# Two weight quarters for the first batch before the second batch, first weights at the head of the queue, blocks of 512 and 384

## The chip, the cores and the metric

The kernel runs on one core of one Trainium2 chip. The metric is the device time of one execution in microseconds.

## What is computed

An attention over 32 memory slots per head, whose output passes through two feed-forward layers of width 2048. There are 8 batches of 576 tokens (4608 tokens in all), 8 heads of 64.

```python
def _attn_ref(q, k, v, phi):
    a = softmax over the sequence of phi          # 8 x 8 x 576 x 32
    k_m = einsum('bhsm,bhsd->bhmd', a, k);  v_m = einsum('bhsm,bhsd->bhmd', a, v)
    attn = softmax(q @ k_m.T / 8)                 # over the 32 slots
    return attn @ v_m

x = attn_out as 4608 x 512
h = x @ w1_in;  g = where(h > 0, h, exp(min(h, 0)) - 1);  x = g @ w1_out
h = x @ w2_in;  g = h * clip(h + 3, 0, 6) / 6;            return g @ w2_out
```

All four weights arrive as 64-bit floats, 512 x 2048 or 2048 x 512 each.

## The kernel before

**Units of the first layer.** Each batch is cut into two halves of 288 tokens; a half is a unit `u`, there are 16. The width 2048 is cut into 16 slices of 128, in four quarters of four slices. An item is one slice of one unit: `first(n)` makes six TensorE products into `ph` (L662 to L664), `middle(n)` applies the activation on ScalarE (L671, L673, L680), VectorE (L675) and GpSimd (L682), and `second(n)` makes twelve products into the four banks `acc` (L706). Each product with full precision is three products of high and low parts.

**What an item waits for.** `first` needs the unit's attention weights `a` (high part L592, low part on GpSimd L595) and the folded weights `w` of its batch and quarter: `fold` multiplies the summary of the batch by the quarter of `w1i` (L616), and takes high and low parts (L622, L624). `second` needs the same quarter of `w1o`.

**The weights.** A quarter is four tiles of 1 MB: two of `w1i`, two of `w1o`. `fetch` loads one (L240), `convert` turns 64-bit floats into 32-bit ones: absolute value on ScalarE (L284), scaled low word on ScalarE (L287), four steps on VectorE (L289, L291, L294, L297), a product on GpSimd (L310), and a last addition on VectorE (L312). For `w1o` a high part on ScalarE (L317) and a low part on GpSimd (L321) follow. The very first two tiles are converted in single slices of 512 elements, the others in pairs of 1024.

**The attention of a batch.** `front_first` (batch 0) or `front` makes the exponentials of `phi`; `summary` makes `pkv` (L515), `kvn` (L527), a transposition, and the copies `vt` (VectorE, L537) and `kt` (ScalarE, L539); `scores` (L552) and `softmax` (L568 to L599) give `a`, per half.

**Order of the items.** For the first two batches (units 0 to 3) `items` runs through the quarters, and in each through all four units, so that a new quarter of weights is wanted every 16 items; the sums over quarters are kept in SBUF (L736 to L755). From the third batch on, all 16 slices of a unit follow one another. While layer one runs, the second layer's weights are converted and written back to DRAM (`seven`).

**The second layer** works on blocks of token pairs: `BLOCKS = [464] * 4 + [448]`, each `t` meaning 2t tokens. Seven products per weight tile replace eight; a block makes 14 x 8 groups of six products of `t` columns (`product1`, L858 to L860; `product2`, L885 to L887) and streams its weights anew.

**The order of every engine's instructions** comes from a planner that runs while the program is built. Each task yields pieces with an engine, an estimated cost and the keys and buffer slots they need; every lane has a due time, counted in items; the planner gives an engine the piece with the smallest due time, and fills gaps with others (`Schedule.pick`). The due times come from `first_use` and `AHEAD`. A key `("step", n)` holds a piece back until item `n` has made its first products; the key `("e", 0, 0)` holds it back until the first half of batch 0's exponentials is there. On the chip the order of each engine is fixed; only waits on semaphores remain. All loads are issued by SyncE, in one queue, in the order of the lists `loads` and `fetches`.

Of the kernel before, what the change touches and what calls it, by code (L numbers as in the profile page):

```python
# [36 lines left out]

BLOCKS = [464] * 4 + [448]
NU = len(BLOCKS)
# [9 lines left out]

ORDER = (1, 6, 2, 7, 5, 4, 3)  # L50

READ = 12
# [128 lines left out]
def mixer(ctx, tc, phi_t, phi_n, kv, q_t, w1i, w1o, w2i, w2o, out):  # L181
# [83 lines left out]
    def convert(n, c, name, i, f, how, *keys):  # L265
# [42 lines left out]
        for x in range(m):  # L308
            yield Piece("pool", 1.2)
            pool.tensor_tensor(out=rest[:, x], in0=rest[:, x], in1=highf[:, x], op=ALU.mult)  # L310
        yield Piece("dve", two)
        dve.tensor_tensor(out=top, in0=top, in1=rest, op=ALU.add)  # L312
        drop(n, c)
# [148 lines left out]
    def front_first(b):  # L462
# [8 lines left out]
        for g in range(NG):  # L471
            yield Piece("dve", 0.7, ("pt", b, g))
            pt.append(kept.pop((b, "pt", g)))
            dve.tensor_reduce(out=nmax[:, g:g + 1], in_=pt[g], op=ALU.max, axis=AX.X, negate=True)
            yield Piece("act", 0.76)
            act.activation(out=pt[g], in_=pt[g], func=ACTF.Exp, bias=nmax[:, g:g + 1],
                           accum_out=sums[:, g:g + 1])
            yield Piece("pe", 1.0, slots=("h", "bank"))
            many, few = new("h", [P, SC - 1, P], "pt4"), new("bank", [P, P], "pt1")
            for c in range(SC):  # L480
                n = P if c < SC - 1 else last
                to = many[:, c] if c < SC - 1 else few[:n]
                pe.transpose(to, pt[g][:, c * P:c * P + n], ident)
            give("x")
            give("t")
            to = pn[:, :, g * P:(g + 1) * P]
            yield Piece("dve", 0.65, early=READ)
            dve.tensor_copy(to[:, :SC - 1], many)
            give("h")
            yield Piece("dve", 0.25, early=READ)  # L490
            dve.tensor_copy(to[:last, SC - 1], few[:last])
            give("bank")
            mark("e", b, g)
# [7 lines left out]
    def summary(b, g, whole):  # L501
# [33 lines left out]
        kr, vr = slice(64 * g, 64 * g + 64), slice(64 - 64 * g, 128 - 64 * g)  # L535
        yield Piece("dve", 0.25, early=READ)
        dve.tensor_copy(vt[b % 2][vr], v4[vr])  # L537
        yield Piece("act", 0.25, early=READ)
# [95 lines left out]

    UB = 2 * HV
    items = [(u, f, q) for q in range(NQ) for u in range(UB) for f in range(q * FQ, q * FQ + FQ)]
    items += [(u, f, None) for u in range(UB, NB) for f in range(FC)]
# [203 lines left out]
    def product1(u, j, i):  # L841
# [6 lines left out]
        if after:  # L848
            keys.append((after, u, j))
        yield Piece("pe", 1.375 * t / 512, *keys, slots=(kind,) if begin else ())  # L850
        if begin:
# [17 lines left out]
    def product2(u, i, j):  # L869
# [6 lines left out]
        if after and j == 0:  # L876
            keys += [(after, u, "o", d) for d in range(2)]
        yield Piece("pe", 1.375 * t / 512, *keys, slots=kinds if begin and j == 0 else ())
        if begin and j == 0:
# [163 lines left out]
    swaps, opl, oplows, streams = sch.lane(), sch.lane(), sch.lane(), sch.lane()  # L1043

    def first_use(u, f):
        if u < UB:
            return (f // FQ * UB + u) * FQ + f % FQ
        return u * FC + f

# [9 lines left out]
    for n in range(0, len(order), 2):  # L1059
        src, name, i, f = order[n]  # L1060
        how = dict(w1i="whole", w1o="parts").get(name, "seven")
        begin = UB * FC + 5 * (n - early) if how == "seven" else (i - 1) * UB * FQ
        if n < 2 * FQ:
            pre.append(fetch(n, src, i, f))
        else:
            fetches.add(fetch(n, src, i, f, *([("step", begin - 3)] if begin >= 3 else
                                              [("raw", 6)])))
        for c in [slice(0, 1), slice(1, 2)] if n < SINGLE else [slice(0, 2)]:
            x = f + c.start
            due = begin + 14 if how == "seven" else (  # L1070
                i * UB * FQ + (x if i == 0 or how == "parts" else 0)
                + LATER * (how == "parts") - AHEAD["w_in" if how == "whole" else "w_out"])
            convs[lane % CONVERSIONS].add(
                convert(n, c, name, i, x, how, ("e", 0, 0),
                        *([("step", begin)] if begin >= 0 else [])), due=due)
            lane += 1
    for n, (name, j) in enumerate((name, j) for name in ("w2i", "w2o") for j in range(NJ)):
        sevens[n % len(sevens)].add(seven(name, j), due=UB * FC + 10 * n + 19)

    kvs = [[load_kv_whole(b, n) for n in range(3)] for b in range(2)]  # L1080
    loads.add(load_front(0), kvs[0][0], *pre[:2], *kvs[0][1:], load_q(0, 0), pre[3], pre[2],
              load_q(0, 1), load_front(1), load_q(1, 0), *kvs[1], load_q(1, 1))
    for b in range(B):
        n = (b - 1) * HV * FC
        whole = b < UB // HV
        when = [n + 2, n + 10, n + 18]
        if b == UB // HV:
            when = [2 * UB * FQ, 3 * UB * FQ, 3 * UB * FQ]
        need = first_use(b * HV, 0) - AHEAD["start"] * (b == 0)
# [12 lines left out]
        elif b == 0:  # L1102
            for q in range(NQ):
                for j in range(UB // HV):
                    folds.add(fold(j, q, 1 if j == q == 0 else FQ),
                              due=first_use(j * HV, q * FQ) - AHEAD["fold"])

# [93 lines left out]
```

## Time and profile before

| | us |
|---|---|
| median of 3 runs | 1466.34 |
| all runs | 1465.06, 1466.34, 2794.55 |
| the profiled execution, its own time | 1463.72 |
| its span | 1461.9 |
| TensorE matmul busy | 1414.6 (97%) |
| VectorE busy | 1095.0 (75%) |
| ScalarE busy | 817.2 (56%) |
| GpSimd busy | 458.8 (31%) |

The profiled execution takes 1.8 us more than its span. The shares are means over stages with different limits: layer one's start (to about 250 us), the rest of layer one (to about 758 us), and the second layer. The digits of the page show the shares in 40 slices of 36.5 us each. A profile row of a window gives each engine's busy time with its number of instructions in brackets, and then the granted TensorE clock as a share of 2.4 GHz.

### The profile page before, as it was taken

The numbers are of one execution on the slowest core, as the hardware profiler recorded it, in microseconds if no ns is written. First come the engines' busy times: TensorE is split into PE (matmuls) and PEld (weight loads), VectorE is DVE, ScalarE is ACT, GpSimd is POOL, SyncE is SP. The second block draws the span as 40 slices with busy tenths as digits, with TensorE's granted clock in tenths as the row PEclk, the third lists the DMA queues.
The fourth block names the chain that finished last, engine by engine and source line by source line (L and its number), as shares of the span: only waits on it lengthen the run. The fifth ranks groups of instructions, "written<-read, shape, count | busy, mean of one in ns | idle before, by whom it ended". The sixth has DMA issues, their size and how long they took to land.

```text
span 1461.9 us, 25619 instructions
## 1 busy us (share of the span) xinstructions
PE 1414.6 (97%) x9464; PEld 1283.9 (88%) x9464; DVE 1095.0 (75%) x1785; ACT 817.2 (56%) x1691; POOL 458.8 (31%) x464
## 2 busy tenths in 40 slices
PE   4698999999999999999999999999999999999999
PEld 2588898989999899999998888888888888889998
DVE  5998865677586786767357896789678867986785
ACT  4677775667667676667653454355335534553453
POOL 1678984456557565656420000000000000000000
PEclk7799999999999999999999999999999999999999
DMA  9421215336546455654336468556936783676562
GB/s 363 184 80 71 102 63 178 101 112 236 174 162 204 155 180 178 200 170 167 124 111 239 170 226 338 194 182 222 370 140 209 247 352 131 210 274 270 204 234 117
DMA packets 94221, 279.41 MB, mean 191 GB/s; under 512 B 8976, under 2 KB 50960, under 8 KB 75920
## 3 DMA queue, kind: packets, MB, share of 16 engines
q1 hardware_dynamic: 94096, 277.78, 53.5%
q8 instruction: 74, 1.21, 0.3%
q14 instruction: 51, 0.42, 0.1%
HBM read 229.51 MB, written 48.23 MB: 190 GB/s over the span
## 4 chain that ended last, share of the span: by engine, by line
PE 87%; DVE 4%; issue 3%; POOL 3%; DMA 2%; ACT 1%; SPq 0%; DVEq 0%; ACTq 0%; POOLq 0%
PE acc L706 23%; PE ph L662 5%; PE ph L663 4%; PE ph L664 4%; PE pb L859 3%; PE qb L885 3%; PE qb L886 3%; PE qb L887 3%; PE pb L858 3%; PE pb L860 3%; PE pg L859 2%; PE pa L859 2%; PE qa L885 2%; PE qa L886 2%; PE qg L885 2%
## 5 line engine op out<-in xcount | busy, mean ns | idle before, releaser
L682 POOL TENSOR_TENSOR g<-e,g 128x288 fp32r<-128x288 f32 x256 | 251.4, 988 | 234.0 <-ACT g L680 214.5
L979 ACT CAST goh<-G 128x464 fp32r<-128x464 f32 (+1 forms) x280 | 155.6, 575 | 103.1 <-PE qb L887 46.2
L675 DVE SCALAR_TENSOR_TENSOR e<-e,ph 128x288 f32<-128x288 f32 x256 | 114.4, 449 | 129.8 <-ACT e L673 113.9
L981 DVE TENSOR_TENSOR gol<-G,goh 128x464 fp32r<-128x464 f32 (+1 forms) x280 | 172.7, 636 | 34.2 <-PE qb L886 14.0
L662 PE MATMUL ph<-ahi,wf 128*128 128x288 f32 x512 | 159.3, 311 | 5.2 <-DVE e L675 4.3
L680 ACT CAST g<-e 128x288 fp32r<-128x288 f32 x256 | 109.3, 431 | 90.1 <-DVE e L675 86.0
L947 ACT ACTIVATE e<-c,three 128x464 f32<-128x464 f32 (+1 forms) x120 | 81.9, 682 | 137.6 <-DVE c L924 123.4
L671 ACT ACTIVATE e<-ph 128x288 f32<-128x288 f32 x256 | 104.8, 409 | 95.3 <-PE ph L664 82.3
L663 PE MATMUL ph<-alo,wf 128*128 128x288 f32 x512 | 152.3, 298 | 1.5 <-POOL alo L595 1.4
L664 PE MATMUL ph<-ahi,wf 128*128 128x288 f32 x512 | 152.2, 297 | 0.2 <-DVE wf L624 0.2
L662 PEld LDWEIGHTS ph<-ahi,wf 128*128 128x128 f32 x512 | 96.9, 189 | 37.5 <-issue 14.3
L673 ACT ACTIVATE e<-e 128x288 f32<-128x288 f32 x256 | 114.0, 445 | 7.5
L663 PEld LDWEIGHTS ph<-alo,wf 128*128 128x128 f32 x512 | 97.2, 190 | 2.5 <-POOL alo L595 2.5
L664 PEld LDWEIGHTS ph<-ahi,wf 128*128 128x128 f32 x512 | 97.2, 190 | 0.4 <-DVE wf L624 0.4
L706 PE MATMUL acc<-g,w1o3h 128*128 128x288 f32 x512 | 94.3, 296 | 0.0
L706 PE MATMUL acc<-g,w1o0h 128*128 128x288 f32 x512 | 91.0, 303 | 2.4 <-ACT w1o0h L317 2.4
L706 PE MATMUL acc<-g,w1o1h 128*128 128x288 f32 x512 | 90.4, 297 | 2.4 <-POOL g L682 2.4
L706 PE MATMUL acc<-g,w1o2h 128*128 128x288 f32 x512 | 90.1, 295 | 0.0
L859 PE MATMUL pb<-op,ws 128*128 128x464 f32 (+1 forms) x240 | 89.1, 371 | 0.0
L885 PE MATMUL qb<-goh,ws 128*128 128x464 f32 (+1 forms) x240 | 88.9, 370 | 0.0
L886 PE MATMUL qb<-goh,ws 128*128 128x464 f32 (+1 forms) x240 | 88.9, 370 | 0.0
L887 PE MATMUL qb<-gol,ws 128*128 128x464 f32 (+1 forms) x240 | 88.9, 370 | 0.0
(156 smaller groups left out, 3690.8 us busy)
## 6 DMA issues: line engine op xcount, KB each, us to landing
ws<-w2o SPq DMA_DIRECT2D x70, 1024.0 KB, 5.1
ws<-w2i SPq DMA_DIRECT2D x40, 1024.0 KB, 7.4
ws<-w2i SPq DMA_DIRECT2D x40, 768.0 KB, 7.9
kvc<-in_kv SPq DMA_DIRECT2D x60, 256.0 KB, 5.5
q<-in_q_t SPq DMA_DIRECT2D x32, 288.0 KB, 4.7
x2d<-st SPq DMA_DIRECT2D x32, 288.0 KB, 3.7
raw<-in_w1i SPq DMA_DIRECT2D x8, 1024.0 KB, 8.7
raw<-in_w1o SPq DMA_DIRECT2D x8, 1024.0 KB, 9.3
```

The costliest lines, as they stand in the source:

```text
L662: pe.matmul(ps, whi, xhi, start=begin and c == 0, stop=False)
L663: pe.matmul(ps, whi, xlo, start=False, stop=False)
L664: pe.matmul(ps, wlo, xhi, start=False, stop=close and c == len(passes) - 1)
L675: dve.scalar_tensor_tensor(out=e, in0=e, scalar=-1.0, in1=ps, op0=ALU.add, op1=ALU.max)
L682: pool.tensor_tensor(out=lo, in0=e, in1=hi.bitcast(F32), op=ALU.subtract)
L706: pe.matmul(acc[d], w[:, f % FQ, d * P:(d + 1) * P], g[x], start=first, stop=last)
L859: pe.matmul(ps, whi, xlo, start=False, stop=False, **more)
L885: pe.matmul(ps, whi, hi, start=begin and j == 0, stop=False, **more)
L886: pe.matmul(ps, wlo, hi, start=False, stop=False, **more)
L887: pe.matmul(ps, whi, lo, start=False, stop=j == NJ - 1, **more)
L979: act.copy(hi, x)
L981: dve.tensor_tensor(out=lo, in0=x, in1=hi.bitcast(F32), op=ALU.subtract)
```

## The change

- `FIRST` sets the order of quarters (q) and batches (b) for units 0 to 3: (0,0), (1,0), (0,1), (1,1), (2,0), (2,1), (3,0), (3,1). Batch 0 takes quarters 0 and 1 (16 items), then batch 1 takes them, then quarters 2 and 3 go by turns as before. The due times of folds, scores, fronts and conversions follow from it: quarter 1 of the weights is wanted at item 8 and not 16, batch 1 at item 16 and not 8. Quarters 2 and 3 are wanted at items 32 and 48 in both kernels.
- Conversions no longer wait for `("e", 0, 0)`; those of quarter 1 no longer wait for `("step", 0)`.
- The first weight tile is loaded ahead of batch 0's `phi`; the second comes behind `phi` and ahead of all of `k` and `v`.
- The last addition of the conversion of the first two tiles (four single slices) goes from VectorE to GpSimd.
- The four copies of batch 0's exponentials out of PSUM, and the copy `vt` of every batch, go from VectorE to ScalarE.
- `BLOCKS` becomes [512, 512, 512, 384, 384].
- The planner's cost of a group of six products becomes 0.08 + t/400 us instead of 1.375 t/512.

```diff
-BLOCKS = [464] * 4 + [448]
+BLOCKS = [512] * 3 + [384] * 2
...
+FIRST = [(0, 0), (1, 0), (0, 1), (1, 1), (2, 0), (2, 1), (3, 0), (3, 1)]
...
-        yield Piece("dve", two)
-        dve.tensor_tensor(out=top, in0=top, in1=rest, op=ALU.add)
+        if n < 4:
+            yield Piece("pool", 0.5 + 0.7 * m)
+            pool.tensor_tensor(out=top, in0=top, in1=rest, op=ALU.add)
+        else:
+            yield Piece("dve", two)
+            dve.tensor_tensor(out=top, in0=top, in1=rest, op=ALU.add)
...
-            yield Piece("dve", 0.65, early=READ)
-            dve.tensor_copy(to[:, :SC - 1], many)
+            yield Piece("act", 0.65, early=READ)
+            act.copy(to[:, :SC - 1], many)
...
-        yield Piece("dve", 0.25, early=READ)
-        dve.tensor_copy(vt[b % 2][vr], v4[vr])
+        yield Piece("act", 0.25, early=READ)
+        act.copy(vt[b % 2][vr], v4[vr])
...
-    UB = 2 * HV
-    items = [(u, f, q) for q in range(NQ) for u in range(UB) for f in range(q * FQ, q * FQ + FQ)]
+    UB = len({b for q, b in FIRST}) * HV
+    items = [(u, f, q) for q, b in FIRST for u in range(HV * b, HV * b + HV)
+             for f in range(q * FQ, q * FQ + FQ)]
...
-        yield Piece("pe", 1.375 * t / 512, *keys, slots=(kind,) if begin else ())
+        yield Piece("pe", 0.08 + t / 400, *keys, slots=(kind,) if begin else ())
...
+    where = {(u, f): n for n, (u, f, _) in enumerate(items)}
+
     def first_use(u, f):
-        if u < UB:
-            return (f // FQ * UB + u) * FQ + f % FQ
-        return u * FC + f
+        return where[u, f]
+
+    block_use = [min(where[u, q * FQ] for u in range(UB)) for q in range(NQ)]
...
-        begin = UB * FC + 5 * (n - early) if how == "seven" else (i - 1) * UB * FQ
+        begin = UB * FC + 5 * (n - early) if how == "seven" else block_use[i] - 4 * FQ
...
-                i * UB * FQ + (x if i == 0 or how == "parts" else 0)
+                block_use[i] + (x if i == 0 or how == "parts" else 0)
                 + LATER * (how == "parts") - AHEAD["w_in" if how == "whole" else "w_out"])
             convs[lane % CONVERSIONS].add(
-                convert(n, c, name, i, x, how, ("e", 0, 0),
+                convert(n, c, name, i, x, how,
                         *([("step", begin)] if begin >= 0 else [])), due=due)
...
-    loads.add(load_front(0), kvs[0][0], *pre[:2], *kvs[0][1:], load_q(0, 0), pre[3], pre[2],
+    loads.add(pre[0], load_front(0), pre[1], *kvs[0], load_q(0, 0), pre[3], pre[2],
               load_q(0, 1), load_front(1), load_q(1, 0), *kvs[1], load_q(1, 1))
```

## Rows read from the trace of the kernel before

**Rows 1.** The page's slices, engine busy tenths over the span:

```profile
PE   4698999999999999999999999999999999999999
```

**Rows 2.** Line L706 from 50 to 250 us: durations, then first and last start in us:

```profile
L706 PE MATMUL acc<-g,w1o0h x128: 288/295/442, 53.7 to 109.1; 128*128 128x288 f32 x128
...
L706 PE MATMUL acc<-g,w1o1h x128: 288/295/442, 111.6 to 159.0; 128*128 128x288 f32 x128
...
L706 PE MATMUL acc<-g,w1o2h x128: 288/295/401, 160.9 to 205.0; 128*128 128x288 f32 x128
...
L706 PE MATMUL acc<-g,w1o3h x128: 288/295/401, 206.7 to 249.1; 128*128 128x288 f32 x128
```

**Rows 3.** The chain of waits, two steady items: start us, us, what:

```profile
262.54 1.59 PE acc L706 x12
...
264.92 1.59 PE acc L706 x12
```

**Rows 4.** Windows: us; PE, PEld, DVE, ACT, POOL busy us (count), PEclk, DMA share, GB/s:

```profile
5.50:14.40 8.90, 4.45 (x42) 3.27 (x42) 2.59 (x8) 2.96 (x8) 0.00 (x0) 1.00 1.00 389
14.40:24.80 10.40, 5.75 (x66) 2.75 (x66) 7.28 (x17) 4.63 (x9) 2.13 (x2) 0.61 1.03 404
24.80:41.00 16.20, 9.85 (x98) 5.36 (x98) 14.56 (x30) 8.33 (x19) 4.80 (x5) 0.61 1.04 399
41.00:116.20 75.20, 59.75 (x470) 49.84 (x470) 71.64 (x92) 50.06 (x103) 53.39 (x41) 0.89 0.33 124
116.20:205.00 88.80, 83.02 (x665) 77.54 (x665) 75.11 (x100) 65.47 (x141) 80.55 (x69) 0.98 0.20 69
250.00:750.00 500.00, 498.82 (x4310) 466.34 (x4309) 343.95 (x553) 340.52 (x784) 288.00 (x308) 1.00 0.49 163
```

**Rows 5.** PE in order of time: start us, us, instruction, idle time before it:

```profile
31.66 0.61 PE L662 MATMUL ph<-ahi,wf 128*128 128x288 f32 x1
...
53.73 0.93 PE L706 MATMUL acc<-g,w1o0h 128*128 128x288 f32 x4 [0.36 <-ACT w1o0h L317]
...
68.33 0.29 PE L662 MATMUL ph<-ahi,wf 128*128 128x288 f32 x1
```

**Rows 6.** Windows, DVE busy of one tile: two of w1i, two of top, one of z:

```profile
24.80:41.20 16.40, 5.87 (x9) 0.60 1.05 401
...
62.00:89.10 27.10, 14.12 (x10) 0.94 0.12 40
...
41.00:62.00 21.00, 10.48 (x10) 0.69 0.58 231
...
90.00:118.00 28.00, 14.01 (x10) 0.96 0.33 120
...
69.00:91.85 22.85, 9.98 (x14) 1.00 0.21 68
```

**Rows 7.** DVE twice, then POOL, in order of time: start us, us, instruction:

```profile
14.83 0.43 DVE L291 TENSOR_SCALAR w1i<-w1i 128x512 uint32<-128x512 uint32 x1
...
16.81 1.15 DVE L291 TENSOR_SCALAR w1i<-w1i 128x512 uint32<-128x512 uint32 x1
...
16.58 1.09 POOL L310 TENSOR_TENSOR raw<-raw 128x512 f32<-128x512 f32 x1 [14.87 <-DVE raw L297]
```

**Rows 8.** ACT, then PE, in order of time, where a DMA ended the wait:

```profile
12.68 0.67 ACT L284 ACTIVATE w1i<-raw 128x512 f32<-128x512 f32 x1 [3.10 <-DMA raw<-in_w1i]
...
17.92 0.66 PE L515 MATMUL pkv<-kvw,pn 128*32 128x128 f32 x8 [4.48 <-DMA kvw<-in_kv]
```

**Rows 9.** Windows of the second layer, blocks of 464 and of 448 tokens:

```profile
900.00:1000.00 100.00, 100.00 (x478) 89.49 (x478) 77.87 (x134) 43.79 (x77) 0.00 (x0) 1.00 0.60 220
1340.00:1440.00 100.00, 100.00 (x496) 92.66 (x495) 80.78 (x141) 44.90 (x81) 0.00 (x0) 1.00 0.53 201
```

**Rows 10.** Groups from 760 to 1462 us: xcount | busy us, mean ns | idle:

```profile
L981 DVE TENSOR_TENSOR gol<-G,goh 128x464 fp32r<-128x464 f32 x224 | 139.0, 639 | 24.9 <-PE qb L886 10.1 <-ACT goh L979 5.2 <-PE qb L887 4.0
...
L981 DVE TENSOR_TENSOR gol<-G,goh 128x448 fp32r<-128x448 f32 x56 | 33.7, 622 | 9.3 <-PE qb L886 3.9 <-PE qg L886 2.9 <-ACT goh L979 1.1
```

More of the change, by code (lines that the diff above doesn't have):

```diff
@@ L486, in front_first @@
             to = pn[:, :, g * P:(g + 1) * P]
-            yield Piece("dve", 0.65, early=READ)
-            dve.tensor_copy(to[:, :SC - 1], many)
+            yield Piece("act", 0.65, early=READ)
+            act.copy(to[:, :SC - 1], many)
             give("h")
-            yield Piece("dve", 0.25, early=READ)
-            dve.tensor_copy(to[:last, SC - 1], few[:last])
+            yield Piece("act", 0.25, early=READ)
+            act.copy(to[:last, SC - 1], few[:last])
             give("bank")
@@ L535, in summary @@
         kr, vr = slice(64 * g, 64 * g + 64), slice(64 - 64 * g, 128 - 64 * g)
-        yield Piece("dve", 0.25, early=READ)
-        dve.tensor_copy(vt[b % 2][vr], v4[vr])
+        yield Piece("act", 0.25, early=READ)
+        act.copy(vt[b % 2][vr], v4[vr])
         yield Piece("act", 0.25, early=READ)
@@ L877, in product2 @@
             keys += [(after, u, "o", d) for d in range(2)]
-        yield Piece("pe", 1.375 * t / 512, *keys, slots=kinds if begin and j == 0 else ())
+        yield Piece("pe", 0.08 + t / 400, *keys, slots=kinds if begin and j == 0 else ())
         if begin and j == 0:
@@ L1078, in mixer @@
         sevens[n % len(sevens)].add(seven(name, j), due=UB * FC + 10 * n + 19)
-    kvs = [[load_kv_whole(b, n) for n in range(3)] for b in range(2)]
-    loads.add(load_front(0), kvs[0][0], *pre[:2], *kvs[0][1:], load_q(0, 0), pre[3], pre[2],
+    kvs = [[load_kv_whole(b, n) for n in range(3)] for b in range(UB // HV)]
+    loads.add(pre[0], load_front(0), pre[1], *kvs[0], load_q(0, 0), pre[3], pre[2],
               load_q(0, 1), load_front(1), load_q(1, 0), *kvs[1], load_q(1, 1))
+    for b in range(2, UB // HV):
+        loads.add(load_front(b), *kvs[b], load_q(b, 0), load_q(b, 1))
     for b in range(B):
@@ L1087, in mixer @@
         if b == UB // HV:
-            when = [2 * UB * FQ, 3 * UB * FQ, 3 * UB * FQ]
+            when = [UB * FC - 32, UB * FC - 16, UB * FC - 16]
         need = first_use(b * HV, 0) - AHEAD["start"] * (b == 0)
@@ L1102, in mixer @@
         elif b == 0:
[L1103 to L1106, printed above, removed]
+            for q, j in FIRST:
+                folds.add(fold(j, q, 1 if j == q == 0 else FQ),
+                          due=first_use(j * HV, q * FQ) - AHEAD["fold"])
     swaps.add(swap(), due=n2 - 16)
```

## The prediction

> **What bounds the kernel now.** I read the page's slices first: TensorE (PE) is nearly full from the fourth slice on, and what it lacks it lacks in the first three and a little in the rest of the first 250 us [rows 1]. The windows say the same with numbers: 250 to 750 us hold 498.8 us of PE work in 500 [rows 4], and the second layer 100.0 in 100 [rows 9]. So PE sets the pace in four fifths of the span, and no edit that leaves its work alone can gain there. The change leaves that work alone: the same items, the same products.
>
> The loss lies in the start. An undisturbed item takes 264.92 - 262.54 = 2.38 us [rows 3], a quarter of the weights serves 16 items, so 38.1 us. The second products over the four quarters begin at 53.7, 111.6, 160.9 and 206.7 us and the last begin at 249.1 [rows 2]: the quarters take 57.9, 49.3, 45.8 and about 42.5 us, which is 19.8, 11.2, 7.7 and 4.4 us more than 38.1 (a few us of each are folds and scores, also PE work). Ahead of them lie 53.7 us, with the first product of item 0 at 31.66 [rows 5].
>
> Who is late there? Item 0 has its first products at 31.66, its second only at 53.73, and that waits for the high part of w1o, which is converted [rows 5]. From 24.8 us on VectorE (DVE) is the engine that is always at work: 14.56 of 16.2 us, then 71.64 of 75.2 (95%), then 75.11 of 88.8 beside GpSimd (POOL) with 80.55 of 88.8 [rows 4]. The reader is to see two things: the start is a queue of DVE work, and DVE has room only before it, 2.59 us busy of the 8.9 between 5.5 and 14.4, 7.28 of 10.4 after that [rows 4]. So what counts is how much DVE work moves ahead of 24.8 us or off DVE. An order of the items alone moves none.
>
> **First weights ahead of all.** ScalarE gets the first tile at 12.68 us, having waited for nothing else [rows 8]; the queue moves 389 to 404 GB/s by then [rows 4], so each 1 MB ahead of it costs 2.6 to 2.7 us, and phi (0.6 MB) and the first part of k and v (1 MB) stood ahead of it. At the head it should land at about 5 to 6 us, the second tile by 11. The key on the exponentials is gone, so the four single conversions can run in the idle time from 6 to 20 us. In the old order 5.87 us of their DVE work (9 instructions) stands behind 24.8 us, in the middle of the queue [rows 6]. That moves out whole: **-5.9 us**. Bounds: 0 if they stay where they are; -5.9 is all there is.
>
> The price of it is on phi, which moves 2.7 us back. Its chain ends in `pkv`, which waits for k and v, landing just before 17.92 [rows 8]. The bytes ahead of the last of k and v are the same, so the wait for them covers phi's delay. If the cover went, at most the 2.7 us would come back; I take 0.
>
> **Work taken off DVE.** The four last additions are among the conversions; two of them were inside the 5.9 us. On POOL an operation of this shape takes 1.09 us, and POOL is idle at 5.5 to 14.4 and 2.13 us busy in the next 10.4 [rows 4, 7], so they are hidden. The copies of the exponentials leave DVE in time that it had to spare: 0. ScalarE takes them with 2.96 us busy of 8.9 [rows 4]. Of the `vt` copies two (batch 1) stand in the queue; the nearest row of like size is a slice of 512 at 0.43 us [rows 7], so they are worth between 0 and 0.9 us: **-0.6**. For later batches PE hides both.
>
> **What POOL's work costs DVE.** The same instruction of DVE took 0.43 us alone and 1.15 us when a POOL operation ran from 16.58 to 17.67 [rows 7]. Four more POOL operations can so cost DVE 0 to 4 x 0.72 = 2.9 us; in the idle time I take 0. On this the Trainium skill, page SBUF — State Buffer, section "Who interferes with whom", says that a VectorE instruction with two SBUF inputs, or in a two-port mode, and a GpSimd instruction that reads SBUF exclude each other for the whole instruction. The trace agrees with the 1.15 us. By the rule alone each moved addition (two SBUF inputs on either engine) shifts the conflict rather than removing it.
>
> **Batch 0 takes two quarters.** By item 16 DVE must have done the same: quarter 0's w1o (10.48 us), quarter 1's w1i (14.12), quarter 1's w1o (14.01), batch 1's softmaxes (9.98) [rows 6]. The old order wanted batch 1 at item 8 and quarter 1 at item 16; the new one wants 28.1 us of conversion at item 8 and batch 1 at item 16. In between PE has 8 items, 19 us. Early items come sooner: w1o of quarter 0 no longer stands behind batch 1's front and the rest of the w1i slices, so item 0's second products could start near 41 us, 12.7 us earlier, and items 4 to 7 long before 68.33 [rows 5]. Then PE waits for quarter 1 as it waited for batch 1 before. Counting DVE's queue from 24.8 us: before, it took until about 116 us (16.2 + 75.2 of time with 86.2 of work [rows 4]); now 86.2 - 5.9 - 0.6 = 79.7 of work. The waits in it were 5.2 us; with more of the first quarter ready I expect a us less: **-1**. Nothing later changes: quarters 2 and 3 keep their items, their release, and the window in which POOL is 91% and DVE 85% busy [rows 4]. The lead is carried through to the second layer.
>
> **Blocks of 512 and 384.** 478 matmuls of 464 columns in 100 us are 209.2 ns each, 496 of 448 are 201.6 [rows 9]. The step is 0.475 ns a column, so a line through both gives 232.0 at 512 and 171.2 at 384. Per matmul index: 4 x 209.2 + 201.6 = 1038.4 before, 3 x 232.0 + 2 x 171.2 = 1038.4 after. There are 672 per block, so 0 us; an error of 2 ns in the 512 would be 3 x 672 x 2 ns = 4 us either way. DVE has a fixed part: 639 ns at 464 and 622 at 448 [rows 10], so 554 at 384 against 171.2 x 6 of PE. Its share of the last block's windows rises from 81% [rows 9] by (554/171.2)/(622/201.6) = 1.05 to 85%: still below PE. The smaller last block shortens the tail by some 0.1 to 0.5 us: **-0.3**. The new cost formula changes a plan in which PE is full anyway: 0.
>
> **Sum.** 5.9 + 0.6 + 1 + 0.3 = 7.8 us, from the profiled execution's 1463.7 (span 1461.9 and 1.8 around it) to 1455.9. The two close runs shown are 1.3 and 2.6 us above it; with 1.5 us the forecast is 1457.
>
> **Rivals.**
> - *PE, not DVE, was the one that waited in order.* If early items come 12.7 us sooner and quarter 1's overrun (11.2 us) goes too because all of quarter 1 is ready by then, the gain is up to 24 us: 1441; half of that second part gives 1447. For it: the 22 us between first and second products of item 0. Against: DVE at 95%. Chance 0.17.
> - *Nothing arrives.* DVE and POOL exclude each other more often, since conversions now run beside more POOL work: 2.9 us for the additions and the gain of idle time lost to longer instructions later; POOL, at 91% from 116 to 205 us, sets the end of the conversions and gives the lead back. 1462 to 1466. The Trainium skill's rule above would lead here. Chance 0.23.
> - *Batch 1 becomes the wait, and it is slower.* Its front, summary and softmaxes are due behind quarter 1's 28.1 us of conversion. If the planner puts all of them behind, the chain (9.98 us of softmax, as much again for front, summary, scores and low parts, some 8 us until an item's second products) starts at about 90 us and item 16 gets its second products near 117 instead of 111.6; with the lead gone that is 6 to 10 us more: 1472 to 1476. It decides if batch 1's first softmax begins after 100 us. The same if the reordered loads delay `pkv`. Chance 0.14.
> - *The shorter blocks let streams or DVE stall PE*, 10 us or more: 1466 to 1480. Against: DMA share 0.53 to 0.60 in layer two [rows 9]. Chance 0.04.
>
> **How the numbers follow.** The forecast (a gain of 4 to 13 us, 1452 to 1461) has 0.42. The range has to hold 8 in 10: the forecast, most of the first rival and the second make 0.78, so I take 1444 to 1468; the forecast's own range is 1452 to 1461. Two per cent is 29 us, about what a measurement of this kernel can tell from no change. Faster by that needs more than the first rival's whole 24 us: 0.05. Slower by that needs a layer-two stall over many blocks or a much worse plan: 0.03. The rest, 0.92, is the same.
>
> **What would show it.** Right: DVE busy for most of 6 to 20 us, no w1i of single slices after 25 us; item 0's second products near 41 us; first use of w1o's quarters 2 and 3 some 7 to 8 us earlier than 160.9 and 206.7; layer two's matmuls of 512 near 232 ns and no gaps. Wrong: item 0's first products later than 33 us (phi's delay not covered), `scores` of batch 1 ending a PE wait, PE below 100 in 100 in a block of 384. The forecast fails most easily if the queue of DVE is not what carries the lead: then the quarters' first uses move by other amounts than 8 us.

## The result, and the profile after

The median went from 1465.94 to 1449.04 us (1448.69 to 1450.54), a ratio of 0.9889 with a 95% interval of 0.9869 to 0.9908. That is inside the predicted range of 1444 to 1468 and better than the forecast's own range of 1452 to 1461: the gain is 16 to 17 us where the sum had 7.8 and the forecast of 1457 us some 9. The ratio leaves out one slow execution of the kernel before, of 2794.55 us. The profiled execution took 1448.69 us; its span and the page's slices of PE are these (the slices answer to [rows 1]; only the first two are far from full):

```profile
span 1446.9 us, 25631 instructions
...
PE   4599999999999999999999999999999999999998
```

The span fell by 1461.9 - 1446.9 = 15.0 us. Two lines mark where. The first product of the second layer is the first start of `pa`, the last is the last start of `qg` (each row: number, shortest/median/longest ns, first and last start in us, forms). Of the kernel before:

```profile
L858 PE MATMUL pa<-op,ws x160: 361/370/375, 753.5 to 1385.8; 128*128 128x464 f32 x128, 128*128 128x448 f32 x32
...
L887 PE MATMUL qg<-gol,ws x160: 362/368/376, 869.4 to 1458.0; 128*128 128x464 f32 x128, 128*128 128x448 f32 x32
```

and of the kernel after:

```profile
L865 PE MATMUL pa<-op,ws x160: 333/389/500, 748.1 to 1381.1; 128*128 128x512 f32 x96, 128*128 128x384 f32 x64
...
L894 PE MATMUL qg<-gol,ws x160: 334/389/389, 873.1 to 1442.8; 128*128 128x512 f32 x96, 128*128 128x384 f32 x64
```

The second layer begins at 748.1 instead of 753.5 us: **-5.4 us** from the start. From its first to its last product it takes 694.7 instead of 704.5 us: **-9.8 us**. What follows the last product is 4.1 instead of 3.9 us. So the larger part came from the term that the prediction put at nothing.

The windows of after stand in the same stretches and columns as [rows 4] and [rows 9]:

```profile
5.50:14.40 8.90, 3.93 (x38) 3.03 (x42) 7.46 (x12) 7.75 (x16) 3.53 (x3) 1.00 1.03 396
14.40:24.80 10.40, 5.09 (x94) 2.29 (x86) 9.31 (x16) 2.11 (x6) 6.05 (x5) 0.88 1.04 408
24.80:41.00 16.20, 7.72 (x76) 4.24 (x76) 12.94 (x23) 8.51 (x18) 5.42 (x5) 0.61 1.04 401
41.00:116.20 75.20, 59.47 (x498) 52.21 (x499) 66.97 (x92) 51.95 (x107) 53.48 (x47) 0.85 0.37 136
...
900.00:1000.00 100.00, 100.00 (x443) 82.81 (x442) 77.77 (x123) 42.87 (x71) 0.00 (x0) 1.00 0.55 205
1340.00:1440.00 100.00, 100.00 (x578) 100.00 (x578) 78.83 (x156) 46.48 (x93) 0.00 (x0) 1.00 0.60 232
```

VectorE is busy 16.8 of the 19.3 us before 24.8 (9.9 before), as wanted, and then less: 12.94 + 66.97 = 79.9 us of work from 24.8 to 116.2, where the prediction had 79.7. But its idle time there rose from 5.2 to 11.5 us, 1.1 us of the 6.3 before 64.7 us and the rest behind it (the stretch is 91.4 us in both, so less work in it is more idle time). The block of 384 keeps PE at 100.00 in 100 with 578 matmuls where 448 had 496.

The quarters' first uses answer to [rows 2]:

```profile
L713 PE MATMUL acc<-g,w1o0h x138: 288/295/608, 45.6 to 250.0; 128*128 128x288 f32 x138
...
L713 PE MATMUL acc<-g,w1o1h x128: 288/295/402, 91.7 to 154.5; 128*128 128x288 f32 x128
...
L713 PE MATMUL acc<-g,w1o2h x128: 288/295/402, 156.1 to 199.6; 128*128 128x288 f32 x128
...
L713 PE MATMUL acc<-g,w1o3h x128: 288/295/403, 202.8 to 245.3; 128*128 128x288 f32 x128
```

(The last start of `w1o0h` belongs to the third batch.) Quarter 0 begins 8.1 us earlier than before, quarter 2 4.8 and quarter 3 3.9. Between them the lead was gone once: item 16, now batch 1's first, has its second products at 111.61 us, as the old item 16 had. PE in order of time (start us, us, instruction, idle time before it):

```profile
15.50 0.43 PE L521 MATMUL pkv<-kvw,pn 128*32 128x128 f32 x8 [0.53 <-DMA kvw<-in_kv]
...
31.92 0.61 PE L669 MATMUL ph<-ahi,wf 128*128 128x288 f32 x1
...
58.30 1.33 PE L713 MATMUL acc<-g,w1o0h 128*128 128x288 f32 x4 [4.42 <-POOL g L689]
64.73 1.96 PE L622 MATMUL pw<-w1i,vt 64*32 64x512 f32 x16 [5.10 <-DVE w1i L318]
66.62 0.61 PE L669 MATMUL ph<-ahi,wf 128*128 128x288 f32 x1
...
111.61 0.86 PE L713 MATMUL acc<-g,w1o0h 128*128 128x288 f32 x4
```

`pkv` now waits 0.53 us for k and v and starts at 15.50 instead of 17.92 [rows 8], but the first products of item 0 still come at 31.92 (31.66 in [rows 5]). Then PE stands for 4.42 us before 58.30 and for 5.10 us before 64.73. VectorE in the same time:

```profile
48.12 0.68 DVE L291 TENSOR_SCALAR w1i<-w1i 128x1024 f32<-128x1024 f32 x1
...
59.25 0.68 DVE L299 TENSOR_SCALAR raw<-w1i 128x1024 uint32<-128x1024 uint32 x1
59.86 0.74 DVE L586 TENSOR_REDUCE sm<-z 128x18 f32<-128x576 f32 x1
```

From 48.12 to 59.9 us it converts two pieces of quarter 1's `w1i`; only at 59.86 does it go on with the sums of the softmax of batch 0's second half, which items 4 to 7 need (their first products come at 66.62). The wait before 64.73 ends with the last addition of the second piece, for a fold of quarter 1 that stands ahead of items 4 to 7 in PE's order.

From 66.62 us on the roles change. The stretch up to item 16, before, then after (columns as above):

```profile
90.00:111.60 21.60, 20.48 (x157) 18.08 (x150) 20.43 (x26) 15.82 (x36) 16.56 (x13) 1.00 0.35 122
...
90.00:111.60 21.60, 21.60 (x177) 19.54 (x176) 17.98 (x31) 16.61 (x37) 14.15 (x15) 1.00 0.44 165
```

Before, neither engine is full (PE 95%, VectorE 95%); after, PE is full and VectorE has 3.6 us to spare. PE works off items 4 to 15, for which it stood still earlier, and VectorE's idle time in that stretch costs nothing.

### The profile page after: what moved, and what is told of

It reads as the page before. It is cut to its first block, busy times and chain, and to the rows that moved or that the text cites. A ratio compares the mean times of both kernels' runs of the same rounds, so it can differ in the third digit from the quotient of the medians.

```text
span 1446.9 us, 25631 instructions
## 1 busy us (share of the span) xinstructions
PE 1397.2 (97%) x9464; PEld 1261.7 (87%) x9464; DVE 1081.6 (75%) x1761; ACT 822.3 (57%) x1711; POOL 459.0 (32%) x468
## 4 chain that ended last, share of the span: by engine, by line
PE 86%; DVE 1%; POOL 1%; DMA 1%; issue 1%; ACT 1%; SPq 0%; DVEq 0%; ACTq 0%; POOLq 0%
PE acc L713 23%; PE ph L669 4%; PE ph L671 4%; PE ph L670 4%; PE qb L894 3%; PE pb L865 3%; PE pb L866 3%; PE pb L867 3%; PE qb L892 3%; PE qb L893 3%; PE pa L865 2%; PE qg L894 2%; PE qa L894 2%; PE pg L865 2%; PE pg L866 2%; PE qa L892 2%
## 5 line engine op out<-in xcount | busy, mean ns | idle before, releaser
L986 ACT CAST goh<-G 128x512 fp32r<-128x512 f32 (+1 forms) x280 | 155.6, 576 | 96.6 <-PE qb L894 38.7
L988 DVE TENSOR_TENSOR gol<-G,goh 128x512 fp32r<-128x512 f32 (+1 forms) x280 | 171.8, 635 | 24.4 <-PE qb L893 11.8
L954 ACT ACTIVATE e<-c,three 128x512 f32<-128x512 f32 (+1 forms) x120 | 81.9, 682 | 134.5 <-DVE c L931 114.8
L865 PE MATMUL pb<-op,ws 128*128 128x512 f32 (+1 forms) x240 | 88.1, 367 | 0.0
L866 PE MATMUL pb<-op,ws 128*128 128x512 f32 (+1 forms) x240 | 88.1, 367 | 0.0
L867 PE MATMUL pb<-op,ws 128*128 128x512 f32 (+1 forms) x240 | 88.1, 367 | 0.0
L892 PE MATMUL qb<-goh,ws 128*128 128x512 f32 (+1 forms) x240 | 88.1, 367 | 0.0
```

Of the source, the lines that this page charges most:

```text
L865: pe.matmul(ps, whi, xhi, start=begin and k == 0, stop=False, **more)
L866: pe.matmul(ps, whi, xlo, start=False, stop=False, **more)
L867: pe.matmul(ps, wlo, xhi, start=False, stop=k == 1, **more)
L892: pe.matmul(ps, whi, hi, start=begin and j == 0, stop=False, **more)
L986: act.copy(hi, x)
L988: dve.tensor_tensor(out=lo, in0=x, in1=hi.bitcast(F32), op=ALU.subtract)
```

## The experiments

The first five ask what a block's size is worth, the other seven what carries the start. Ratios are against the kernel before on the same chip, and runs from different chips are compared by them; its medians there were 1464.57 us (for the first four), 1463.75 (the order alone, the loads alone, all work back, the softmax earlier) and 1464.27 (the others). "Item 16" is the seventeenth in a kernel's own order.

**Blocks alone.** The kernel before with one line changed:

```diff
-BLOCKS = [464] * 4 + [448]
+BLOCKS = [512] * 3 + [384] * 2
```

> The kernel before with blocks of 512, 512, 512, 384, 384 and nothing else changed. Theory A (the columns of a matmul set its price: 226.7 ns at 512 and 173.4 at 384 in the trace of after, against 209.7 at 464 and 202.7 at 448 in that of before): 672 x (4 x 209.7 + 202.7 - 3 x 226.7 - 2 x 173.4) = 672 x 14.6 ns, or 9.8 us less than before, about 1456. Theory B (the prediction's: a matmul's price is linear in its columns, and layer two was faster in the changed kernel because of what the start handed it): within 1 us of before, 1465, with layer two of 704 us.

Measured: 1455.34 us, 0.9939 [0.9924, 0.9954], so 9.2 us less. The same two rows:

```profile
L858 PE MATMUL pa<-op,ws x160: 333/389/496, 754.0 to 1387.1; 128*128 128x512 f32 x96, 128*128 128x384 f32 x64
...
L887 PE MATMUL qg<-gol,ws x160: 334/389/389, 879.1 to 1448.8; 128*128 128x512 f32 x96, 128*128 128x384 f32 x64
```

The layer begins at 754.0, as before (753.5), and takes 694.8 us instead of 704.5. The whole gain lies inside the layer. The full change has 694.7 there, with the planner's new cost of a group as well, so that new cost is worth nothing, as the prediction had it.

**All but the blocks.** The kernel after with the old line:

```diff
-BLOCKS = [512] * 3 + [384] * 2
+BLOCKS = [464] * 4 + [448]
```

> The changed kernel with the old blocks of 464 and 448. Theory A: it loses the 9.8 us again, 1459, and keeps the 5 to 6 us of the start. Theory B: it stays near 1449 to 1450.

Measured: 1460.18 us, 0.9969 [0.9957, 0.9982], 4.4 us less than before; the layer begins at 750.0 and takes as long as before. So the start is worth 4.4 us here. The ratio of the full change over that of the blocks alone, 0.9889/0.9939, would leave it 7.3, to some 4 us either way by the two intervals; the trace of the full change says 5.4. The prediction's start terms add up to 7.5: the two better values lie below it, the third doesn't tell them apart.

**The price of a size.** The kernel before with other sizes, each block long enough to count matmuls in (one execution each, 1460.1 us for the first list and 1470.46 for the second):

```diff
-BLOCKS = [464] * 4 + [448]
+BLOCKS = [512, 496, 480, 432, 384]
```

> The kernel before with blocks of 512, 496, 480, 432 and 384: the price of a matmul at five sizes in one execution. A straight line of 2.4 columns a ns with 13.3 ns on top (which 384 and 512 lie on) would give 226.7, 220.0, 213.3, 193.3 and 173.3 ns. Theory A1 (only multiples of 128 are on the line): 496, 480 and 432 lie 2 to 4 ns above it. Theory A2 (464 and 448 are exceptions for another reason, such as where their tiles lie): the three are on the line.

Windows inside the five blocks, in order (us; PE, PEld, DVE, ACT, POOL busy us (count), PEclk, DMA share, GB/s):

```profile
775.00:890.00 115.00, 115.00 (x509) 95.20 (x509) 98.35 (x155) 54.72 (x91) 0.00 (x0) 1.00 0.52 179
910.00:1040.00 130.00, 130.00 (x584) 109.25 (x583) 104.36 (x168) 57.95 (x98) 0.00 (x0) 1.00 0.58 206
1060.00:1190.00 130.00, 130.00 (x599) 112.11 (x598) 104.47 (x174) 58.55 (x103) 0.00 (x0) 1.00 0.61 217
1205.00:1320.00 115.00, 115.00 (x589) 110.42 (x588) 91.87 (x168) 52.01 (x98) 0.00 (x0) 1.00 0.66 236
1335.00:1440.00 105.00, 105.00 (x606) 104.87 (x605) 80.48 (x159) 46.13 (x92) 0.00 (x0) 1.00 0.70 267
```

```diff
-BLOCKS = [464] * 4 + [448]
+BLOCKS = [448, 416, 400, 368, 352, 320]
```

> The kernel before with six blocks of 448, 416, 400, 368, 352 and 320. The line gives 200.0, 186.7, 180.0, 166.7, 160.0 and 146.7 ns. Theory A1: all lie 2 to 4 ns above it. Theory A2: all on it. Either way one block more adds 672 x 13.3 ns = 9 us of fixed cost, so the time should be 1466 to 1478.

```profile
780.00:880.00 100.00, 100.00 (x486) 90.81 (x485) 84.67 (x151) 48.13 (x89) 0.00 (x0) 1.00 0.57 195
900.00:1005.00 105.00, 105.00 (x559) 104.17 (x558) 86.32 (x164) 49.70 (x96) 0.00 (x0) 1.00 0.67 241
1025.00:1130.00 105.00, 105.00 (x583) 105.00 (x582) 86.11 (x168) 50.25 (x99) 0.00 (x0) 1.00 0.71 257
1145.00:1240.00 95.00, 95.00 (x569) 95.00 (x569) 77.85 (x164) 45.77 (x96) 0.00 (x0) 1.00 0.76 277
1260.00:1350.00 90.00, 89.14 (x556) 88.85 (x555) 74.22 (x163) 44.06 (x95) 0.00 (x0) 1.00 0.78 281
1365.00:1445.00 80.00, 80.00 (x546) 80.00 (x545) 61.58 (x143) 35.44 (x80) 0.00 (x0) 1.00 0.84 322
```

PE's busy time over its count, and what is left of it after columns divided by 2.4 GHz (the granted clock is 1.00 in all of them):

| columns | 320 | 352 | 368 | 384 | 400 | 416 | 432 | 448 | 464 | 480 | 496 | 512 |
|---|---|---|---|---|---|---|---|---|---|---|---|---|
| ns a matmul | 146.5 | 160.3 | 167.0 | 173.1 | 180.1 | 187.8 | 195.2 | 201.6 | 209.2 | 217.0 | 222.6 | 225.8 |
| over columns / 2.4 | 13.2 | 13.7 | 13.6 | 13.1 | 13.4 | 14.5 | 15.2 | 14.9 | 15.9 | 17.0 | 15.9 | 12.5 |

The 384 is the mean of the windows of this run and of after, the 512 that of this run's 225.9 and of after's 225.7, the 448 and 464 are from [rows 9]; 448 as the first block above takes 205.8 instead. So 512, 384 and the sizes up to 400 leave 12.5 to 13.7 ns, and all between 416 and 496 leave 14.5 to 17. A window counts the matmuls that it cuts at its two ends as whole ones, so all these values are a little low, by 0.1 to 1.1 ns. Taken from one start to the next over whole blocks, the same traces give 226.7 at 512, 173.4 at 384, 209.7 at 464 and 202.7 at 448, which leave 13.4, 13.4, 16.4 and 16.0 ns; the two groups are then 13.3 to 14.0 and 15.3 to 17.5, and the order stays. It is not a matter of multiples of 128 alone, since 320, 368 and 400 are as good as 384. The two sizes of the kernel before both lie in the dear stretch.

**The place of the tiles.** The tiles of the old sizes at the distance of the new ones (operands and PSUM banks 512 wide, the first 464 or 448 used; three more allocations in the same way):

```diff
-            ops[u, i] = new(HERE[i], [P, 2, 2, t], f"op{i}", F32R)
+            ops[u, i] = new(HERE[i], [P, 2, 2, 512], f"op{i}", F32R)[:, :, :, :t]
```

> The kernel before, blocks of 464 and 448, with the operands and results of layer two's matmuls kept in tiles of 512 columns of which the first 464 or 448 are used, so that they start where those of blocks of 512 do. If the number of columns alone sets the price: 209.7 and 202.7 ns as before. If the place of the tiles does: 206.7 and 200.0 ns.

```profile
900.00:1000.00 100.00, 100.00 (x481) 89.90 (x480) 78.26 (x135) 44.80 (x80) 0.00 (x0) 1.00 0.61 219
1340.00:1430.00 90.00, 90.00 (x446) 83.42 (x445) 74.09 (x130) 41.26 (x75) 0.00 (x0) 1.00 0.57 218
```

207.9 ns at 464 by this window (209.2 before) and 201.8 at 448 (201.6): 1.3 of the 3 ns by which 464 lies too high. From start to start it is 208.9 for 209.7, and 202.7 both times, so 0.8 of the 3. The time of this one execution was 1461.4 us, 2.9 below its set's median, where the blocks alone gave 9.2. So tiles that lie as those of 512 do don't make 464 cheap. That the rest goes with the number of columns alone is not shown: 448 as the first block of the second list costs 4 ns more than as the last block of the kernel before, so something besides the columns counts there, and only this one placing was tried. Why, no run shows.

**The order alone.** The kernel before with the new order of quarters and batches and the due times that follow from it; loads, keys, engines and blocks are the old ones (the planner's new cost of a group is in this kernel and the next, 1.24 instead of 1.25 us at 464):

```diff
+FIRST = [(0, 0), (1, 0), (0, 1), (1, 1), (2, 0), (2, 1), (3, 0), (3, 1)]
...
-    items = [(u, f, q) for q in range(NQ) for u in range(UB) for f in range(q * FQ, q * FQ + FQ)]
+    items = [(u, f, q) for q, b in FIRST for u in range(HV * b, HV * b + HV)
+             for f in range(q * FQ, q * FQ + FQ)]
```

> The kernel before with the order FIRST and the due times that follow from it, and nothing else: old order of loads, the wait for the exponentials kept, all additions and copies on VectorE, old blocks. Theory S1 (VectorE's queue carries the lead, the order alone moves no work): within 1.5 us of before, 1463 to 1466. Theory S2 (the lead of the changed kernel, which is nothing at item 16 and 4.5 us at item 32, comes from the order: quarter 1 is converted earlier): 1459 to 1461.

Measured: 1467.28 us, 1.0026 [1.0015, 1.0037]. By itself the order costs 3.5 us, more than either theory had. Item 0's second products come earlier, at 48.6 us, but item 16 at 118.0 and quarter 2 here (same columns as above):

```profile
L713 PE MATMUL acc<-g,w1o1h x128: 288/295/402, 98.4 to 160.5; 128*128 128x288 f32 x128
...
L713 PE MATMUL acc<-g,w1o2h x128: 288/295/402, 162.6 to 207.1; 128*128 128x288 f32 x128
```

at 162.6 instead of 160.9; the second layer begins at 755.2.

**Loads and early conversions alone.** Weights first and no wait for the exponentials, in the old order, with the old blocks, and with copies and additions on VectorE. Against the kernel before:

```diff
-                convert(n, c, name, i, x, how, ("e", 0, 0),
+                convert(n, c, name, i, x, how,
...
-    loads.add(load_front(0), kvs[0][0], *pre[:2], *kvs[0][1:], load_q(0, 0), pre[3], pre[2],
+    loads.add(pre[0], load_front(0), pre[1], *kvs[0], load_q(0, 0), pre[3], pre[2],
```

> The kernel before with the first weights loaded ahead and converted without the wait for the exponentials; old order of items, all additions and copies on VectorE, old blocks. S1: the 5.9 us of conversion leave the queue, 1457 to 1460. S2: VectorE's spare time is used but the items still wait in the same places, 1463 to 1466.

Measured: 1459.71 us, 0.9971 [0.9961, 0.9981], 4.0 us less.

```profile
L713 PE MATMUL acc<-g,w1o1h x128: 288/295/442, 106.5 to 156.0; 128*128 128x288 f32 x128
...
L713 PE MATMUL acc<-g,w1o2h x128: 288/295/401, 157.8 to 201.6; 128*128 128x288 f32 x128
```

Item 16 comes 5.1 us earlier (106.5 for 111.6), quarter 2 3.1, the second layer 3.4 (750.1). VectorE's queue moved by the same amount: the first step of a piece of the third pair of `w1i` tiles begins at 105.08 instead of 110.09 us. This is the prediction's mechanism, seen by itself: in the old order VectorE is still the fuller engine up to item 16 (20.51 of 21.6 us from 90.0 to 111.6, PE 18.14).

**The work back on VectorE.** After, with the four additions and all copies (the exponentials and `vt`) on VectorE again; below it after with the additions alone back:

```diff
-        if n < 4:
+        if n < 0:
             yield Piece("pool", 0.5 + 0.7 * m)
             pool.tensor_tensor(out=top, in0=top, in1=rest, op=ALU.add)
...
-            yield Piece("act", 0.65, early=READ)
-            act.copy(to[:, :SC - 1], many)
+            yield Piece("dve", 0.65, early=READ)
+            dve.tensor_copy(to[:, :SC - 1], many)
...
-        yield Piece("act", 0.25, early=READ)
-        act.copy(vt[b % 2][vr], v4[vr])
+        yield Piece("dve", 0.25, early=READ)
+        dve.tensor_copy(vt[b % 2][vr], v4[vr])
```

> The changed kernel (1449.0) with the four additions and the copies of the exponentials and of vt back on VectorE. The prediction's value for them: 0.6 us lost, 1449 to 1450. If they keep the first conversions out of the queue, some of their 2.7 us (additions) and 1.9 us (copies) come back: 1451 to 1454. If a moved addition only shifts the conflict between the two engines: 1447 to 1449.

```diff
-        if n < 4:
+        if n < 0:
             yield Piece("pool", 0.5 + 0.7 * m)
             pool.tensor_tensor(out=top, in0=top, in1=rest, op=ALU.add)
```

> The changed kernel with the four additions back on VectorE and the copies still on ScalarE. Both together gave back 2.7 us. If it is the additions: 1451 to 1452. If it is the copies: 1448.5 to 1449.5. Halves: 1450 to 1450.5.

Measured: 1451.76 us, 0.9922 [0.9907, 0.9937], with everything back, and 1449.15 us, 0.9893 [0.9878, 0.9908], with the additions back. The additions are worth nothing that can be measured. The copies are probably worth about 3 us (1451.76 - 1449.15 = 2.6 from two chips; by the ratios 4.2; the intervals touch), which the prediction had at 0 and 0.6; the traces go the same way, with quarter 2 at 160.4 us with everything back and at 154.1 with the additions back. Exponentials and `vt` were not moved apart. In the first the wait before the first fold of a whole piece is longer than after's 5.1 us (us in total, times, longest; of 24 to 112 us):

```profile
PE pw L622 <- DVE w1i L318: 6.8, 1, 6.8
```

But that is not the loss: with the additions back the same wait is 13.7 us long, and the kernel is as fast as after.

**The softmax earlier.** After, with the scores and the softmax of batch 0's second half due as early as those of the first, which takes away the wait before 64.73:

```diff
-    due = first_use(b * HV + hf, 0) - AHEAD["scores"] - AHEAD["start"] * (b == hf == 0)
+    due = first_use(b * HV + hf, 0) - AHEAD["scores"] - AHEAD["start"] * (b == 0)
```

> The changed kernel with the second half's scores and softmax of batch 0 due 20 items earlier, so ahead of the conversion of quarter 1. In the changed kernel VectorE makes 14 instructions of that conversion between the two parts of this softmax, items 4 to 7 begin at 66.6 us, and TensorE stands from 59.6 to 64.7 us. If this wait is on the path: 3 to 7 us less, 1442 to 1446. If VectorE's total up to item 16 decides (S1): within 1 us, 1448 to 1450.

Measured: 1448.56 us, 0.9900 [0.9885, 0.9915]: the same as after. The wait did not go, it moved. PE in order of time and the quarters:

```profile
49.59 0.58 PE L669 MATMUL ph<-ahi,wf 128*128 128x288 f32 x1 [6.69 <-DVE e L682]
...
63.48 0.61 PE L669 MATMUL ph<-ahi,wf 128*128 128x288 f32 x1 [6.04 <-DVE e L682]
```

```profile
L713 PE MATMUL acc<-g,w1o0h x140: 288/295/442, 52.6 to 249.6; 128*128 128x288 f32 x140
...
L713 PE MATMUL acc<-g,w1o1h x128: 288/295/401, 91.0 to 154.0; 128*128 128x288 f32 x128
...
L713 PE MATMUL acc<-g,w1o2h x128: 288/295/401, 155.8 to 199.7; 128*128 128x288 f32 x128
```

Item 0's second products come at 52.6 instead of 45.6 us, item 16 at 111.6 as in after, quarter 2 0.3 us earlier. Which of two jobs of VectorE comes first decides where PE waits, and not when the quarter is through: from 90.0 us to item 16 PE is full here too (21.60 of 21.60 us). The granted clock does not decide it either: it is 1.00 from 24.8 to 45.0 us and 0.89 to 64.7 here, 0.58 and 0.67 in after, and item 16 comes at the same time.

**All but the order.** After with the old order:

```diff
-FIRST = [(0, 0), (1, 0), (0, 1), (1, 1), (2, 0), (2, 1), (3, 0), (3, 1)]
+FIRST = [(0, 0), (0, 1), (1, 0), (1, 1), (2, 0), (2, 1), (3, 0), (3, 1)]
```

> The changed kernel (1449.0) with the old order of the quarters: every batch pair takes a quarter before the next one; all else as changed. The order alone cost 3.5 us on the kernel before, and item 16 came 6.4 us later. Theory S3 (it costs the same beside the other edits): 1444 to 1447. Theory S4 (the order is needed once the first weights are early, because they come into their own only if batch 0 goes on): 1450 to 1453.

Measured: 1455.12 us, 0.9934 [0.9917, 0.9951]: the blocks' gain and nothing from the start, which is outside both theories.

```profile
L713 PE MATMUL acc<-g,w1o1h x128: 288/295/442, 114.1 to 161.1; 128*128 128x288 f32 x128
...
L713 PE MATMUL acc<-g,w1o2h x128: 288/295/401, 162.9 to 206.6; 128*128 128x288 f32 x128
```

Item 16 comes at 114.1, quarter 2 at 162.9, the second layer at 754.0. Yet the loads alone, in this same order, gave 4.0 us; together with the moved copies and additions they give none. The longest waits of 24 to 112 us, first of this kernel, then of the loads alone:

```profile
POOL g L689 <- ACT g L687: 22.5, 5, 8.5
```

```profile
POOL g L689 <- ACT g L687: 13.2, 6, 6.3
```

GpSimd stands 22.5 instead of 13.2 us for the `g` that ScalarE makes, behind ScalarE's other work. That this is what costs the 4 us is argued, not shown.

**The old order with the softmax earlier.** The last kernel with the one line of the softmax's due time as above:

```diff
-FIRST = [(0, 0), (1, 0), (0, 1), (1, 1), (2, 0), (2, 1), (3, 0), (3, 1)]
+FIRST = [(0, 0), (0, 1), (1, 0), (1, 1), (2, 0), (2, 1), (3, 0), (3, 1)]
...
-    due = first_use(b * HV + hf, 0) - AHEAD["scores"] - AHEAD["start"] * (b == hf == 0)
+    due = first_use(b * HV + hf, 0) - AHEAD["scores"] - AHEAD["start"] * (b == 0)
```

> Old order of the quarters as in e9_old_order, and batch 0's second scores and softmax due 20 items earlier as in e8_softmax_first. The latter was worth 0.5 us in the new order. If it is worth the same: 0 to 1 us below e9_old_order. If it puts off the conversion of w1o that item 0 waits for: 1 to 3 us above.

Measured: 1449.24 us, 0.9895 [0.9880, 0.9910].

```profile
L713 PE MATMUL acc<-g,w1o1h x128: 288/295/402, 110.4 to 154.2; 128*128 128x288 f32 x128
...
L713 PE MATMUL acc<-g,w1o2h x128: 288/295/401, 156.0 to 200.8; 128*128 128x288 f32 x128
```

Neither expectation held. Item 16 at 110.4, quarter 2 at 156.0, the second layer at 748.3: as good as after, in the old order. And the line that does nothing in the new order (the run before the last two) is worth 5.9 us in the old one. So the new order is not needed for the gain. What the good plans have in common no run shows: it is not the lack of long waits, since the kernel with the additions back has one of 13.7 us on PE. None of these kernels is measurably better than after: 1448.56, 1449.15 and 1449.24 us have ratios of 0.9900, 0.9893 and 0.9895, within each other's intervals and after's.

## Why the prediction was right and where it was wrong

**The second layer: the step that failed.** "A line through both" sizes gave 232.0 ns at 512 and 171.2 at 384, and so 0 us, with 4 us either way. Measured are 225.8 and 173.1 (672 x (4 x 209.2 + 201.6 - 3 x 225.8 - 2 x 173.1) ns = 10 us by the windows, 9.8 from first to last product). The 0 was in the method and not in the rows: before and after have the same number of matmuls and the same sum of columns (4 x 464 + 448 = 3 x 512 + 2 x 384 = 2304), so any straight line, of whatever slope, gives 0. The layer's gain is what the price departs from a line. The slope of that line, 0.475 ns a column, was a weak warning: one column a cycle at 2.4 GHz would be 0.417 ns (from 384 to 512 the runs show 0.41 to 0.42), so the difference between 448 and 464 held something besides columns (part of that slope was the cut matmuls of the windows: from start to start it is 0.44). A third size stood in the rows too: an item of 18 matmuls of 288 columns takes 2.38 us [rows 3], 132.2 ns each, where the line gives 125.6. Bounds from what each row leaves over columns / 2.4 (12.2 ns at 288, 15.9 at 464) would have been 225.5 to 229.2 at 512 and 172.2 to 175.9 at 384, that is -12 to +1 us. On the same price the Trainium skill, page TensorE: Matmul & The Clock Gate, section "Wait — 56ns, not 53.3ns?", states columns over 2.4 GHz and about 2.5 ns for matmuls back to back. The trace doesn't agree for these matmuls, each of which has a weight load of its own: in the second layer 13.3 ns from start to start at the best, and 17.5 at 480 columns. By that rule, a straight line too, the change of blocks would have been worth 0.

That the time still lies inside the range is luck: 9.8 us came from a term put at 0 with 4 us either way, the start gave less than its terms, and the range reached down to 1444 for the sake of another mechanism, the first rival's.

**VectorE's room before 24.8 us: right.** The first conversions ran there, none of a single slice of `w1i` is left behind 24.8 us, and the work left in its queue to 116.2 us is what the sum said, though it took as long. In the old order this alone gave 4.0 us for the 5.9 of the sum, and 5.1 at item 16.

**"A us less" of waits: wrong in sign, and the queue was not what set item 16.** VectorE's idle time grew by 6.3 us in the full change, and the lead at item 16 was nothing. But only 1.1 us of it lies before 64.7 us; from 90.0 to 111.6 us it is PE that is full. The prediction counted VectorE's queue up to item 16 and left out that PE, kept waiting up to 64.73 us, at last for quarter 1's `w1i`, then had items 4 to 15 still to do. The lead came back between items 16 and 32: from 111 to 160 us PE's longer waits add up to 2.7 us instead of 5.5 (before, 2.4 of them for a `g` of GpSimd), and the granted clock is 1.00 instead of 0.96. It is 4.8 us at quarter 2, 3.9 at quarter 3 and 5.4 at the second layer.

**Copies and additions.** The additions at 0 were right. The copies at 0 and 0.6 were probably too low: about 3 us, with intervals that touch. That what stands behind them in VectorE's fixed order makes the difference is argued, not shown.

**The order.** "An order of the items alone moves none" of the work: so it was, but the price was left out. Alone it costs 3.5 us. The wait that the prediction expected, for quarter 1 in place of batch 1, came: 118.0 us at item 16 with the order alone, 111.6 with everything.

**phi behind the first weights: right.** k and v were there 2.4 us sooner, not later, and the first products of item 0 moved by 0.3 us.

**What was to be seen.** Quarters 2 and 3 were to come 7 to 8 us earlier: 4.8 and 3.9. Item 0's second products near 41 us: 45.6. `scores` of batch 1 ended no PE wait, and PE was full in the blocks of 384. There `gol` took 555 ns where 554 was expected, and VectorE was busy 79% and not 85.

**The rivals.** PE as the one that waits (1441 to 1447) did not give its gain, though the time came near: the start gave 5.4 us and not 17 or more. The experiment with the earlier softmax shows that taking one of PE's waits away gains nothing while VectorE's queue up to 64 us stays as long; behind that PE itself, full, set item 16. That nothing arrives is refuted at the start by the 4.0 us of the loads alone, but its mechanism is there: the same VectorE instruction of a single slice takes 0.69 us at 8.32 and 1.67 us at 11.02, beside a moved addition that GpSimd runs from 10.78 to 12.13. Batch 1 as the wait did not decide: the first maximum of its softmax begins at 84.69 us, before the limit of 100. Shorter blocks stalled nothing.

**What stays open.** That the effects do not add up is shown: -4.0 (loads), +3.5 (order), together with the moved work -4.4, and without the order nothing. Why the moved copies and additions cost in the old order is argued from GpSimd's waits only; each edit changes the whole list that the planner writes, and no run moved a copy without that. The start also differs between executions of one plan: after and the kernel with the old blocks have the same order on VectorE, ScalarE and GpSimd up to 738 us, and began the second layer at 748.1 and 750.0 us, so 2 us of any one trace's lead say little.

## What to carry to other kernels

Before costing a tile size, write each known size as columns over the clock plus a remainder: where the remainders differ, a line through two sizes is no price, and the bounds come from the smallest and the largest remainder. Where a planner writes fixed orders for engines that wait in order, a sum of work in one queue gives the gain's size to a few us only, since a moved instruction changes the whole list: measure the parts alone and in pairs, and look which engine is full in each stretch before calling another one's idle time a loss.

## What the hardware showed that was not expected

The remainder over columns / 2.4 rises from 13.4 ns at 400 columns to 17.0 at 480 and falls back to 12.5 at 512, and at 448 it was 14.9 in one place of the program and 19.1 in another (by the windows).

A different first transfer changed the rate of the first 5 us of loads. GB/s in 40 slices of 0.65 us from 0 to 26 us, before, then after:

```profile
GB/s 0 0 43 237 365 360 101 296 265 280 384 306 416 441 425 466 416 429 350 406 397 397 391 391 384 392 396 424 435 411 419 429 441 416 359 415 400 382 388 440
```

```profile
GB/s 0 0 139 113 315 416 403 338 385 393 472 429 466 318 350 391 397 394 394 391 391 372 397 388 400 394 443 455 416 454 403 403 416 394 363 397 386 412 394 378
```

With phi and then k and v at the head, the slices from 3.9 to 6.5 us run at 101 to 296 GB/s; with 1 MB of weights at the head at 338 to 403. By 16.25 us that adds up to 5.49 instead of 5.16 MB, 0.8 us at 400 GB/s. It repeats: from 3.9 to 4.55 us the six kernels with the old first loads run at 101 to 275 GB/s, the eight with the new ones at 403 to 416. The last of k and v came 2.4 us sooner; the rest of that no run here splits.
